# Maxima steps of 256 and 512 keys in two periods, an earlier routing block on VectorE, and late weight steps three products later

## The chip, the cores and the metric

The kernel runs on one core of one Trainium2 chip. The metric is device microseconds for one execution of the whole program; every number below is in microseconds (us) unless marked ns.

## What is computed

A routed attention feeds a two-layer network. The reference, cut to what matters:

```python
batch, n_heads, seq, head_dim = (4, 8, 768, 64);  n_clusters = 16      # attention
n_tokens, d_model, d_ff = (3072, 512, 2048)                            # network
q_assign = argmax(einsum('bhsd,hcd->bhsc', q / |q|, c / |c|))          # k_assign likewise
mask   = q_assign[:, :, :, None] == k_assign[:, :, None, :]
scores = where(mask, q @ k.T / 8, -1e9);  scores -= max(scores, axis=-1)
attn   = exp(scores) / (sum(exp(scores)) + 1e-9)
x = (attn @ v)  as (B*S, H*D)
h = x @ w_in;  g = h * erf(softplus(h));  out = g @ w_out
```

## The kernel before

**Two stages.** The attention takes a little over 400 us; the network the rest. Both are laid out so that TensorE (PE) always has a next matmul in its queue, and the order of the instructions on every engine is the order in which the Python code issues them: all engines go through a wrapper that keeps program order. Since that wrapper records every instruction, the profile gives line L62 to all of them, and they are told apart by engine and by tile names.

**Attention in periods.** The 32 heads are taken as 16 pairs `p`. One pair has 12 blocks of 128 keys by 384 queries: two halves of the queries, six key blocks each. `period(p, i)` for `i` = 0 to 5 does two of these blocks, `u` and `u+1`. In each period PE computes the float32 products of queries and keys (`products`, into the PSUM tiles `sc`, two buffers), adds the bfloat16 mask pass with the shift (`scores`, tiles `qm` and `km`), ScalarE (ACT) takes the exponential into `pr` (`curve`), GpSimd (POOL) adds up the rows (`accumulate`, into parts of `more_out`), and PE multiplies by the values (`attend`, into the PSUM tiles `turned`).

**Maxima one half pair ahead.** The shift is a bound on the row maximum, found half a pair earlier by `maxima_step`: for one block `t` of 128 queries, PE multiplies bfloat16 copies of queries and keys (`kv`, `qv`), adds the mask pass (`km`, `qm`), both into the one PSUM tile `wide`, and VectorE (DVE) reduces each row to its maximum (`nmx`). A block's 768 keys are split over two steps of 384 keys each; since two heads lie side by side, one reduction reads 768 elements. Each period has two steps. The first stands at the front of the period, before `products`; of the second, the `kv`/`qv` pass stands behind `products`, and the `km`/`qm` pass between `scores(u)` and `scores(u+1)`, on other rows of the array than these. `wide` has one buffer: a step's first matmul waits until the reduction of the step before has read it. The steps of blocks `t` = 0 and 1 of pair `p+1` fall into the periods `i` = 3 and 4 of pair `p`.

**What else VectorE has in periods 3 and 4.** In period 3, `similarities(p+2)` has PE multiply queries and keys with the cluster centres, and `choose(p+2)` turns the result into one-hot rows: a transpose into `sims`, a maximum over 16 clusters whose result goes into unused columns of the PSUM tile of block `u+1` (`sc`), and a comparison with that maximum (`hot`); the last transpose (`hotT`) follows in period 0 of the next pair. PE's products of the next period need that `sc` tile, so they wait for `hot`. In the same period stands part of a weight conversion: the network's weights arrive as 64-bit words and are turned into float32 in steps (`size_and_rest`, `bounded`, `sign`, `shifted`, `summed`). `bounded` and `shifted` are VectorE instructions over 512 elements on the same tile, `sign` is ScalarE's, `summed` GpSimd's, after which the next transfer is issued from the SyncE queue. The step `n1 = 2p - 1` passes through period 3 while it is below 22 (`N_EARLY`), that is in pairs 1 to 11. Pairs 0 to 13 have a `choose`. In period 4, `divide` has three parts for the half that has just ended: `den`, then the sum of each of two column halves `k` = 0, 1 in place in `turned`, then the product `x` that leaves for memory.

In short, VectorE's queue from the second reduction of period 3 to the first of period 4 reads, in pairs 1 to 11: reduction, `bounded`, `sims`, `shifted`, maximum, `hot`, reduction.

**The network.** Its products are made by `block`: seven products per block (a scheme with seven multiplications of half-size matrices), each four matmuls into a PSUM `bank`, of which there are six at first and eight after the last `divide`. After each product, VectorE or ScalarE adds the bank into `g`, and one entry of the list `aside_work` is issued. `hidden(0, 0)` is the first stage of the network, 28 products; its list begins with the last ten weight steps' first four (`all_weights(0, 4)`), whose data come by transfers that can start only when the attention's tiles are released; then eight GpSimd sums (`out_forms`). After its first seven products, `finish_attention` runs the last `divide`. What is left in the list at the end is issued by `finish_aside`.

Of the kernel before, what the change touches and what calls it, by code (L numbers as in the profile page):

```python
# [14 lines left out]
ALU = mybir.AluOpType  # L15
ACT = mybir.ActivationFunctionType
AX = mybir.AxisListType
PSUM = bass.MemoryType.PSUM

P = 128  # L20
B, H, S, D = 4, 8, 768, 64
# [4 lines left out]
HW = S // 2  # L26
QW = HW // 2
TW = QW + 2
HJ = NJ // 2
HP = H // 2  # L30
NPAIR = B * HP
# [39 lines left out]
def kernel(  # L71
# [125 lines left out]
    for base, pattern, sign, op, fill in (  # L197
# [5 lines left out]
            out=first, in_=first, compare_op=op, fill=fill, base=base, pattern=pattern,  # L203
# [42 lines left out]
    def bounded(n):  # L246
        w = w_steps[n][0]
        ve.tensor_scalar(out=w, in0=w, scalar1=2.0, scalar2=None, op0=ALU.max)
# [5 lines left out]
    def shifted(n):  # L254
        w = w_steps[n][0].bitcast(U32)
        ve.tensor_scalar(out=w, in0=w, scalar1=3, scalar2=None, op0=ALU.logical_shift_left)
# [8 lines left out]
    for e in range(2):  # L265
        for n in range(2):
            r = e * D + n * Q
# [112 lines left out]
    def maxima_step(p, i, sm=wide, behind=False):  # L380

        st = pairs[p]
        nmx = maxima[p % 2]
        t, half = divmod(i, 2)

        def passes(a, b, start, rows):
            for e in range(2):
                r = slice(e * D + rows.start, e * D + rows.stop)
                te.matmul(
                    sm[:, e, 0:HW], lhsT=st[a][r, t * P : (t + 1) * P],  # L390
                    rhs=st[b][r, half * HW : (half + 1) * HW], start=start, stop=not start,
                )

        passes("qv", "kv", True, slice(0, D))
        if behind:
            yield
        passes("qm", "km", False, slice(Q, D) if behind else slice(0, D))
        if behind:
            yield
        ve.tensor_reduce(  # L400
            out=nmx[:, :, t, half], in_=sm[:, :, 0:HW], axis=AX.X, op=ALU.max, negate=True
        )
        if i in (NJ - 1, 2 * NJ - 1):
            h = i // NJ
            ve.tensor_reduce(
                out=lowest[h][:, :, ::D].rearrange("p t e -> p e t"),
                in_=nmx[:, :, h * HJ : (h + 1) * HJ], axis=AX.X, op=ALU.min,
            )
            turns.append((p, h))
# [82 lines left out]
    def divide(u):  # L492

        p, half, _ = units[u]
        st = pairs[p]
        av = st["av", half]

        psum = turned[1 - half][:, 0:QW]
        for g in range(4):
            te.matmul(psum[g * Q : (g + 1) * Q], lhsT=minus, rhs=st["acc", half][:, g], start=True, stop=True)  # L500

        if u + 1 < len(units):
            inv = routep.tile([P, QW], F32, name="inv")
            den = routep.tile([P, QW], F32, name="den")
        else:
            inv, den = part_of(0, 4 * HW, QW), part_of(1, 0, QW)
        ae.activation(out=inv, in_=psum, func=ACT.Ln, bias=alleps, scale=-1.0)
        ae.activation(out=inv, in_=inv, func=ACT.Exp, scale=-1.0)
        yield
        ve.scalar_tensor_tensor(  # L510
            out=den, in0=psum, scalar=S * EPS, in1=inv, op0=ALU.subtract, op1=ALU.mult
        )
        for k in range(2):
            raw = av[:, k, 0:QW]
            ve.scalar_tensor_tensor(
                out=raw, in0=raw, scalar=av[:, k, QW : QW + 1], in1=inv, op0=ALU.add, op1=ALU.mult
            )
        yield
        x = part_of(0, (2 * p + half) % 4 * HW, HW).rearrange("p (k x) -> p k x", k=2)
        ve.scalar_tensor_tensor(  # L520
            out=x, in0=den.unsqueeze(1).to_broadcast([P, 2, QW]), scalar=2.0, in1=av[:, :, 0:QW],
            op0=ALU.add, op1=ALU.mult,
        )
        b, r = divmod(p, HP)
        for g in range(4):
            rows_of, at = r * P + g // 2 * D, b * S + half * HW + g % 2 * QW
            nc.sync.dma_start(
                out=x_dram[rows_of : rows_of + D, at : at + QW].rearrange("(k r) x -> r k x", k=2),
                in_=x[g * Q : (g + 1) * Q],
            )  # L530
        if half == 1:
            del pairs[p]
        yield
# [72 lines left out]
    aside_work = []  # L606
# [89 lines left out]
    def idle(n):  # L696
        return [lambda: None] * n
# [39 lines left out]
    def run(work):  # L737
        for _ in work:
            pass
# [13 lines left out]
    routing = [iter(())]  # L753
    part = [iter(())]

    def period(p, i):
        u = 2 * NJ * p + 2 * i
        n1, n2 = 2 * p - 1, 2 * p
        early = lambda n: 0 <= n < N_EARLY

        def mask(place):
            which = (MASKS if p else FIRST_MASKS).get((i, place))
            if which:
                return masks(p + 1, *which, turned[0 if i in (0, 5) else 1], place > 1, ve if place == 3 else ae)
            return lambda: None

        if u > 0:
            for which in turns if i in (0, 3) else ():
                turn(*which)
                turns.remove(which)  # L770
            step_ahead(u)
        mask(0)()
        next(part[0], None)
        if i == 0 and p:
            run(routing[0])
        if u == 2:
            next(routing[0])
        products(u)
        products(u + 1)
        mask(1)()  # L780
        second = step_ahead(u + 1, True) if u > 0 else iter(())
        next(second, None)
        scores(u)
        next(second, None)
        mask(3)()
        next(second, None)
        next(part[0], None)
        scores(u + 1)
        later = mask(2)
        if i == 3:  # L790
            similarities(p + 2)
            routing[0] = choose(p + 2, sc_of[u + 1][:, 0])
        curve(u)
        later()
        curve(u + 1)
        if u == 0:
            step_ahead(1)
            similarities(1)
            routing[0] = choose(1, turned[0])
            next(routing[0])  # L800
            next(routing[0])
            vectors(1, "q")
            vectors(1, "k")
        if i == 0 and early(n1 - 1):
            bounded(n1 - 1)
            shifted(n1 - 1)
            sign(n1 - 1)
        elif i == 1 and early(n1):
            size_and_rest(n1)
        elif i == 3 and early(n1):  # L810
            bounded(n1)
            sign(n1)
        elif i == 5 and early(n2):
            rest(n2)
        for _ in range(min(len(forms), FORMS.get(p, {}).get(i, 0))):
            forms.pop(0)[0]()
        if i == 3:
            next(routing[0], None)
            if early(n1):
                shifted(n1)  # L820
            for _ in range(2):
                next(routing[0], None)
        elif i == 1:
            load(p + 1, "v", v, vp)
            if p == 0:
                run(routing[0])
                transposes(2, "q")
        elif i == 2:
            transposes(p + 2, "k")
        elif i == 4:  # L830
            vectors(p + 2, "k")
            vectors(p + 2, "q")
        elif i == 5:
            transposes(p + 3, "q")
        if u > 0:
            if i == 1 and early(n1 - 1):
                summed(n1 - 1)
            elif i == 4 and early(n1):
                summed(n1)
            for w in (u - 2, u - 1):  # L840
                accumulate(w)
            if i % HJ == 1 and p in POOL_FORMS and forms:
                forms.pop(0)[1]()
            for w in (u - 2, u - 1):
                attend(w)
            if i % HJ == 0:
                part[0] = divide(u - 1)
                next(part[0])
        if i == 3 and early(n2):
            size(n2)  # L850
# [11 lines left out]
    st = pairs[0]  # L862
    st["qT"], st["kT"] = rows[0]["q"], rows[0]["k"]
    ve.transpose(out=st["qT"], in_=st.pop("q").rearrange("p n t -> p (n t)"))
    for e in range(2):
        ve.tensor_copy(
            out=ccT[e * D : (e + 1) * D, :, e * C : (e + 1) * C],
            in_=pct[e * D : (e + 1) * D].rearrange("d (r e c) -> d r e c", e=2, c=C)[:, :, e],
# [7 lines left out]
    for r in (0, D):  # L876
        for half in range(2):
            for e in range(2):
                c = r + half * Q + e * C
                ve.tensor_copy(  # L880
                    out=pick[r : r + D, half, e * D : (e + 1) * D].rearrange("p (n c) -> p n c", n=2)[:, :, 1 : C + 1],
                    in_=first[r : r + D, c : c + C].unsqueeze(1).to_broadcast([D, 2, C]),
# [70 lines left out]
    def all_weights(lo, hi):  # L953
        return sum((weights(n) for n in range(lo, hi)), [])

    out_forms = [right_forms(ge, *w_out_parts(f, 2)) for f in range(0, HF, 2)]
# [10 lines left out]
            del a[:1], b[:1]  # L967
        return work

    aside_work += all_weights(0, 4) + out_forms[0] + out_forms[1]  # L970
    hidden(0, 0, {0: finish_attention})
    finish_aside()
    aside_work += together(idle(2) + gates(0, 0, (0,)), all_weights(4, N_LATE))
# [56 lines left out]
```

## Time and profile before

| what | us |
|---|---|
| median of 3 runs (lowest, highest) | 997.0 (996.87, 997.09) |
| profiled execution: its time | 997.0 |
| profiled execution: span from first to last instruction | 995.3 |
| PE busy in the span | 987.6 |
| DVE, ACT, POOL busy | 700.5, 488.0, 350.3 |
| one pair, first `attend` of period 2 to that of the next pair (window 172.67 to 197.26) | 24.59; DVE busy 20.46 of it |
| the same for pair 12 (320.19 to 344.72) | 24.53; DVE busy 19.91 |

The time of an execution holds 1.7 us that lie around the span. Busy time of PE is modelled from overlapping matmuls, so a share of 99% says that PE is hardly ever without work, and not where it waits: short waits show in the starts of its groups. The granted clock of PE is 1.000 over the whole run.

### The profile page before, as it was taken

The numbers are of one execution on the slowest core, as the hardware profiler recorded it, in microseconds if no ns is written. First come the engines' busy times: TensorE is split into PE (matmuls) and PEld (weight loads), VectorE is DVE, ScalarE is ACT, GpSimd is POOL, SyncE is SP. The second block draws the span as 40 slices with busy tenths as digits, with TensorE's granted clock in tenths as the row PEclk, the third lists the DMA queues.
The fourth block names the chain that finished last, engine by engine and source line by source line (L and its number), as shares of the span: only waits on it lengthen the run. The fifth ranks groups of instructions, "written<-read, shape, count | busy, mean of one in ns | idle before, by whom it ended". The sixth has DMA issues, their size and how long they took to land.

```text
span 995.3 us, 20543 instructions
## 1 busy us (share of the span) xinstructions
PE 987.6 (99%) x8362; PEld 743.0 (75%) x8362; DVE 700.5 (70%) x1347; ACT 488.0 (49%) x659; POOL 350.3 (35%) x237
## 2 busy tenths in 40 slices
PE   8999999999999999999999999999999999999998
PEld 3555555555555555688888888888888888888887
DVE  8888888888888876779676554756475647655653
ACT  3777777777776665575432414150505050505050
POOL 1687878787878888662400000000000000000000
PEclk9999999999999999999999999999999999999999
DMA  9444444444444210331000100010001000000001
GB/s 223 78 110 108 107 110 111 110 113 113 87 94 110 51 35 19 102 106 65 1 12 32 42 1 22 22 43 1 22 22 43 1 21 22 1 1 22 22 1 42
DMA packets 147294, 55.88 MB, mean 56 GB/s; under 512 B 128640, under 2 KB 137088, under 8 KB 147200
## 3 DMA queue, kind: packets, MB, share of 16 engines
q1 hardware_dynamic: 144848, 54.29, 21.5%
q8 instruction: 65, 1.06, 0.4%
q10 hardware_dynamic: 2352, 0.30, 0.2%
q14 instruction: 29, 0.24, 0.1%
HBM read 41.98 MB, written 12.58 MB: 55 GB/s over the span
## 4 chain that ended last, share of the span: by engine, by line
PE 96%; DVE 1%; POOL 1%; DMA 1%; issue 0%; ACT 0%; SPq 0%; ACTq 0%; DVEq 0%; POOLq 0%
PE bank L62 43%; PE turned L62 31%; PE sc L62 16%; PE wide L62 6%; POOL more_out L62 1%; DVE nmx L62 1%; DMA g_more<-in_moe_w_out_dram 0%; DMA in_q<-in_q_dram 0%; DVE sims L62 0%; POOL x_more L62 0%; DVE kT L62 0%; DVE qT L62 0%; ACT pr L62 0%; ACT w_out L62 0%; DVE turned L62 0%
## 5 line engine op out<-in xcount | busy, mean ns | idle before, releaser
L62 POOL TENSOR_TENSOR more_out<-more_out,pr 128x768 f32<-128x768 f32 x128 | 217.0, 1695 | 19.2 <-ACT pr L62 10.5
L62 DVE TENSOR_REDUCE nmx<-wide 128x2 f32<-128x768 f32 x189 | 180.6, 955 | 58.9 <-PE wide L62 57.7
L62 ACT ACTIVATE pr<-sc 128x768 f32<-128x768 f32 x192 | 148.8, 811 | 95.6 <-PE wide L62 91.0
L62 PE MATMUL turned<-pr,in_v 128*32 128x194 f32 x3072 | 145.5, 330 | 0.0
L62 PEld LDWEIGHTS turned<-pr,in_v 128*32 128x32 f32 x3072 | 91.5, 109 | 51.2 <-issue 21.3
L62 DVE TENSOR_TENSOR g<-bank,g 128x256 f32<-128x256 f32 x222 | 89.5, 421 | 53.3 <-PE bank L62 46.4
L62 PE MATMUL bank<-x_own,w_in 128*128 128x256 f32 x424 | 104.7, 380 | 0.8 <-DVE g L62 0.8
L62 PE MATMUL bank<-w_out,g 128*128 128x256 f32 x448 | 103.1, 379 | 0.0
L62 PE MATMUL sc<-qT,kT 64*128 64x384 f32 x528 | 98.3, 484 | 0.0
L62 PEld LDWEIGHTS bank<-w_out,g 128*128 128x128 f32 x448 | 85.1, 190 | 11.6
L62 PEld LDWEIGHTS bank<-x_own,w_in 128*128 128x128 f32 x424 | 80.3, 190 | 12.6 <-DVE g L62 1.2
L62 DVE TENSOR_TENSOR osb<-bank,osb 128x256 f32<-128x256 f32 x87 | 35.4, 419 | 72.8 <-ACT osb L62 25.4
L62 ACT COPY g<-bank 128x256 f32<-128x256 f32 x28 | 10.4, 371 | 153.0 <-PE bank L62 148.5
L62 ACT ACT_TABLE_LOAD x48 | 61.6, 1283 | 45.7 <-DVE g L62 45.0
L62 PE MATMUL bank<-x_more,more_in 128*128 128x256 f32 x296 | 76.0, 379 | 0.0
L62 POOL TENSOR_TENSOR more_out<-pr,pr 128x768 f32<-128x768 f32 x32 | 60.0, 1875 | 28.4 <-ACT pr L62 28.4
L62 PEld LDWEIGHTS sc<-qT,kT 64*128 64x128 f32 x528 | 51.8, 187 | 19.8 <-ACT inv L62 2.3
L62 PE MATMUL wide<-kv,qv 64*128 64x384 bf16 x378 | 64.9, 328 | 1.1 <-ACT km L62 0.6
L62 PEld LDWEIGHTS <-qv 64*128 64x128 bf16 x384 | 26.9, 93 | 51.8 <-issue 35.7
L62 PE MATMUL bank<-more_out,g_more 128*128 128x256 f32 x272 | 64.3, 379 | 0.0
L62 DVE TENSOR_TENSOR g<-a_s,g 128x512 f32<-128x512 f32 x96 | 62.4, 688 | 1.4 <-ACT a_s L62 1.4
L62 PE MATMUL wide<-km,qm 64*128 64x384 bf16 (+1 forms) x378 | 62.5, 327 | 0.0
(170 smaller groups left out, 1667.4 us busy)
## 6 DMA issues: line engine op xcount, KB each, us to landing
x_own<-in_moe_w_in_dram SPq DMA_DIRECT2D x13, 512.0 KB, 4.2
in_v<-in_v_dram SPq DMA_DIRECT2D x32, 192.0 KB, 2.9
x_dram<-more_out SPq DMA_DIRECT2D x128, 48.0 KB, 1.9
x_own<-x_dram SPq DMA_DIRECT2D x6, 1024.0 KB, 5.0
out_dram<-osb SPq DMA_DIRECT2D x23, 256.0 KB, 2.0
in_k<-in_k_dram SPq DMA_DIRECT2D x59, 96.0 KB, 2.6
in_q<-in_q_dram SPq DMA_DIRECT2D x58, 96.0 KB, 2.6
g_more<-in_moe_w_out_dram SPq DMA_DIRECT2D x6, 512.0 KB, 3.3
```

Source lines behind the costliest of these rows:

```text
L62: ins = getattr(self.engine, name)(*args, **kw)
```

## The change

The first 256 keys, in place of 384, go to the first step and the other 512 to the second for query blocks 0 and 1 of every pair but the first; the row maxima are the same. In `divide` of a first half (`half` = 0, always in period 4), the sum of column half 1 moves behind the second maxima step of the period; `divide` of a second half is as before. In period 3 the three parts of `choose` follow one another, and `bounded` and `shifted` follow behind them; `sign` stays in its place on ScalarE. The list of `hidden(0, 0)` begins with three empty entries, so each weight step in it is issued three products later, and the last three GpSimd sums are issued after the 28th product. No instruction is added or taken away, and the queues of POOL and SP keep their order.

```diff
+FIRST_KEYS = {0: 256, 1: 256}
@@ maxima_step
         t, half = divmod(i, 2)
+        to = FIRST_KEYS.get(t, HW) if p else HW
+        keys = slice(to, S) if half else slice(0, to)
+        sm = sm[:, :, 0 : keys.stop - keys.start]
...
                 te.matmul(
-                    sm[:, e, 0:HW], lhsT=st[a][r, t * P : (t + 1) * P],
-                    rhs=st[b][r, half * HW : (half + 1) * HW], start=start, stop=not start,
+                    sm[:, e], lhsT=st[a][r, t * P : (t + 1) * P], rhs=st[b][r, keys], start=start, stop=not start,
                 )
...
         ve.tensor_reduce(
-            out=nmx[:, :, t, half], in_=sm[:, :, 0:HW], axis=AX.X, op=ALU.max, negate=True
+            out=nmx[:, :, t, half], in_=sm, axis=AX.X, op=ALU.max, negate=True
         )
@@ divide
                 out=raw, in0=raw, scalar=av[:, k, QW : QW + 1], in1=inv, op0=ALU.add, op1=ALU.mult
             )
-        yield
+            if k == half:
+                yield
@@ period
         elif i == 3 and early(n1):
-            bounded(n1)
             sign(n1)
...
         if i == 3:
-            next(routing[0], None)
+            for _ in range(3):
+                next(routing[0], None)
             if early(n1):
+                bounded(n1)
                 shifted(n1)
-            for _ in range(2):
-                next(routing[0], None)
@@ before hidden(0, 0)
-    aside_work += all_weights(0, 4) + out_forms[0] + out_forms[1]
+    aside_work += idle(3) + all_weights(0, 4) + out_forms[0] + out_forms[1]
```

## The prediction

> **What bounds the kernel now.** I read the page first, then the waits of PE, then PE and DVE in order of time in a steady pair (pair 6, 172.67 to 197.26), in pair 12, and where the network begins.
>
> ```profile
> PE 987.6 (99%) x8362; PEld 743.0 (75%) x8362; DVE 700.5 (70%) x1347; ACT 488.0 (49%) x659; POOL 350.3 (35%) x237
> PE 96%; DVE 1%; POOL 1%; DMA 1%; issue 0%; ACT 0%; SPq 0%; ACTq 0%; DVEq 0%; POOLq 0%
> ```
>
> The end is PE's: 96% of the chain. So a part of the change counts only if it shortens PE's stream, removes a wait of PE, or makes one. The sum of PE's listed waits is 4.4 us, 0.8 of them inside the network; but a matmul whose predecessor's modelled end hides the gap is not listed, so I looked at starts. Period 4 of pair 6, PE, then DVE from period 3 into period 4:
>
> ```profile
> 182.95 0.34 PE L62 MATMUL wide<-kv,qv 64*128 64x384 bf16 x2
> 183.12 0.33 PE L62 MATMUL wide<-km,qm 64*128 64x384 bf16 x2
> 183.28 1.47 PE L62 MATMUL sc<-qT,kT 64*128 64x384 f32 x8
> ...
> 184.62 0.34 PE L62 MATMUL wide<-kv,qv 64*128 64x384 bf16 x2
> ```
>
> ```profile
> 180.54 0.96 DVE L62 TENSOR_REDUCE nmx<-wide 128x2 f32<-128x768 f32 x1 [0.83 <-PE wide L62]
> 181.42 0.42 DVE L62 TENSOR_SCALAR w_in<-w_in 128x512 f32<-128x512 f32 x1
> 181.75 0.58 DVE L62 STREAM_TRANSPOSE sims<-turned 128x384 f32<-128x384 f32 x1
> 182.25 0.38 DVE L62 TENSOR_SCALAR w_in<-w_in 128x512 uint32<-128x512 uint32 x1
> 182.55 0.55 DVE L62 TENSOR_REDUCE sc<-sims 128x24 f32<-128x384 f32 x1
> 183.14 0.55 DVE L62 TENSOR_TENSOR hot<-sims,sc 128x384 bf16<-128x384 f32 x1
> 183.61 0.95 DVE L62 TENSOR_REDUCE nmx<-wide 128x2 f32<-128x768 f32 x1
> ```
>
> The first reduction was released by PE (0.83 idle before it); from there DVE runs without a gap to the reduction at 183.61, which ends at 184.56, and PE's second `wide` group starts at 184.62: 0.05 us after. In pair 12, without conversion, the products take 332.09 - 330.80 = 1.29 and not 1.34:
>
> ```profile
> 328.06 0.96 DVE L62 TENSOR_REDUCE nmx<-wide 128x2 f32<-128x768 f32 x1 [0.83 <-PE wide L62]
> 329.04 0.58 DVE L62 STREAM_TRANSPOSE sims<-turned 128x384 f32<-128x384 f32 x1
> 329.73 0.56 DVE L62 TENSOR_REDUCE sc<-sims 128x24 f32<-128x384 f32 x1
> 330.33 0.55 DVE L62 TENSOR_TENSOR hot<-sims,sc 128x384 bf16<-128x384 f32 x1
> ```
>
> So pairs 1 to 11 already lose 0.06 in period 4 (24.59 against 24.53 a pair): DVE is just late there, and this is the one place of the steady pair where PE meets DVE. The reader should also see the starts: independent neighbours start 0.08 before the end shown of the one ahead (181.42 against 180.54 + 0.96), a dependent one 0.03 after it (`hot`, 183.14), and the pair `sims`, maximum stands 0.69 apart in pair 12, 0.11 after the transpose's end.
>
> **Steps of 256 and 512, on PE.** Passes of 384 columns start 0.16 apart (183.12, 183.28), so a column costs 0.417 ns, 128 columns 0.053. The first step has two passes one after the other: -0.107. In the second step the `kv` pass stands alone: +0.053. Its `km` pass runs beside the scores on other rows, with 0.42 from its start to `attend` (180.10, 180.53): 0.21 of streaming is covered; uncovered it would be +0.053. So a period gains 0.053, if nothing waits. The shorter pass must still cover the loading of the products' float32 weights: two loads for the same rows start 108 ns apart when they are late (183.843 and 183.951 in the trace), and the pass is 107 ns: nothing, at most 0.08 a period by the row of 187 ns for such a load. I take nothing.
>
> The Trainium skill ("TensorE: Matmul & The Clock Gate", LDWEIGHTS) prices a load by its columns over 1.2 GHz, 107 ns for 128, whatever the type: by it the sum is the same as mine, by the 187 ns row 0.08 more a period where DVE isn't late anyway.
>
> **The same on DVE.** Rows of 768 and 384 elements (0.955, 0.551) give 1.05 ns an element: 512 take 0.69, 1024 take 1.22. The two together are as before, but the long one stands in front of the chain. Its start stays at 180.54: PE's second step begins 0.107 earlier, and both its passes are 0.053 longer.
>
> **Routing first.** From the 1024 reduction's start, with pair 12's spacings: 0.98 + 0.27 to `sims`, 0.69 to the maximum, 0.60 to `hot`, 0.55 to its end: 3.09 (before: 3.15). `bounded` starts 0.08 sooner, at 3.01. `bounded` and `shifted` now follow each other on one tile; in period 0 they do already, and the row below says 0.88 for both:
>
> ```profile
> 194.59 0.88 DVE L62 TENSOR_SCALAR w_in<-w_in 128x512 f32<-128x512 f32 x2
> ```
>
> They end at 3.89, the 512 reduction starts at 3.81 and ends at 4.50, where before it was 184.56 - 180.54 = 4.02. So the order costs about 0.2, two independent starts turned into dependent ones plus the wait handling at `sims`, and the long reduction 0.27, of which the short one gives its 0.27 back only at its own end: PE's second group starts at 180.54 + 4.50 + 0.05 = 185.09, 0.47 later than before, though PE could be there at 184.41. Queued behind: `den`, the reduction of the second step, `x`; the products that `hot` holds up are covered by this wait.
>
> Two more terms follow in the pair. The `kv` pass of 512 comes behind the wait: +0.05. And moving one sum behind the second reduction does let that start when PE is ready rather than behind two sums, but the sum and `x` (0.42 and 0.54, dependent) now end after it: the first reduction of period 5 starts some 0.13 later than PE allows, of which PE's slack takes about half: +0.06. Together +0.58 a pair, times 11 pairs: **+6.4**. Bounds: if a dependent start cost nothing more than an independent one, the short reduction would end at 4.02 as before: +0.11 a pair, +1.2. If `bounded` and `shifted` each pay 0.11 rather than 0.03: +0.7 a pair, +7.7. I take 0.58, since every spacing is a row of the same instructions in the same order. POOL's `summed` waits for `shifted` and comes 1.0 later, the sums behind it too; they run back to back to 193.54 and their reader, the `minus` group, starts at 194.51, so with PE itself 0.58 late 0.5 of cover is left. SP's transfers behind it are needed pairs later.
>
> The Trainium skill ("Advanced Engine Details and Errata", The Read-Write Bubble) says that the memory latency shows between any two VectorE instructions, which would make order free. The trace differs: 0.08 of overlap or a gap of 0.03 to 0.11, by dependence. By the rule the change would come to about no difference; by the rows it is slower.
>
> **Pairs without conversion.** Pairs 0, 12 and 13 have routing alone. The short reduction is ready in time (3.01 + 0.69 + 0.05 = 3.75 against PE at 3.87), but `hot` ends at 3.09 and the products' weights may load 0.12 later, at 3.20 against a natural 2.90. In pair 6 they came 0.20 late for a loss of 0.02; so 0.30 late loses 0.10, and the gain of 0.107 is gone: 0. Pair 14, no routing: -0.11. Bounds for the four: -0.43 to 0.
>
> **Late weight steps.**
>
> ```profile
> 417.23 0.66 ACT L62 ACTIVATE w_out<-g_more 128x512 f32<-128x512 f32 x1 [3.50 <-DMA g_more<-in_moe_w_out_dram]
> 417.93 0.43 DVE L62 TENSOR_SCALAR w_out<-w_out 128x512 f32<-128x512 f32 x1 [3.71 <-ACT w_out L62]
> 418.74 1.13 PE L62 MATMUL bank<-x_own,w_in 128*128 128x256 f32 x4 [0.80 <-DVE g L62]
> ```
>
> DVE's `bounded` waits for ScalarE, ScalarE for the transfer, and behind it the sums that free banks. The PE group before started at 416.81 and needs 4 x 0.216 = 0.86, so it lost 418.74 - 417.68 = 1.06. Three products later the sums of products 2 to 5 are ahead of that wait, and with eight banks after `finish_attention` the next bank needed from behind it is asked for after 420: **-1.06**. Bounds: 0 if it only moves to a later product. The three GpSimd sums left over are issued behind the 28th product and needed some 24 us later: nothing; should the steps meet POOL's sums on DVE, a row of 1.24 for `bounded` at 438.38 says +0.8 for one, hidden behind five banks of slack.
>
> **Sum** for the profiled execution of 997.0 (span 995.3), equal to the median: 997.0 + 6.4 - 0.1 - 1.06 = **1002.2**.
>
> **Rivals.**
> - *Faster, the freed buffer*: the short reduction of period 4 frees `wide` early. Place: PE's second group there; price: the wait of 0.057 goes and 0.107 is gained, 11 x 0.164 = 1.8, with 0.43 and 1.06: 993.7. It decides if the DVE stretch from the long reduction's start to the short one's end is 3.81 or less; all its rows together say 4.50, and even without dependence 4.02. Against it. 8%.
> - *No difference*: dependence costs nothing; +1.2 - 0.1 - 1.06: 997.0. For it: the work on DVE is the same; against: the gaps in pair 12. 11%.
> - *Slower still*: the wait at 417.68 only moves, or returns as one of the dependent sums in the first blocks: 1003.3. It is a part of the slower case.
> - *The change doesn't do what it says*: the order of each queue is the program's, so I leave this out.
>
> **Numbers.** A run of this kernel tells no change from 0.2%, 2.0 us. Forecast with its variants (1000.5 to 1004.4) 81%, hence slower 0.81, same 0.11, faster 0.08. The range reaches below the forecast's own towards the middle case: 999.0 to 1004.5.
>
> **What would show it.** In pairs 1 to 11, period 4: PE's second `wide` group some 0.67 behind the end of its products, the 512 reduction starting 3.8 after the 1024 one; a pair of 25.2 in place of 24.59, pair 14 alone shorter; no wait of PE near 417. Wrong if pairs 1 to 11 take 24.5 or less: then DVE doesn't set period 4; or if the network's beginning still waits.

## The result and the profile after

| | before | changed |
|---|---|---|
| median of 10 runs each (lowest, highest) | 997.10 (996.84, 997.93) | 999.77 (999.52, 1000.48) |
| ratio, 95% interval | | 1.0026 [1.0016, 1.0036] |
| span of the profiled execution | 995.3 | 998.1 |
| first to last `attend` of the attention | 384.99 | 388.82 |
| last `attend` to the last matmul | 582.03 | 580.96 |
| one pair: 1 to 11; 12 and 13; 14 | 24.59; 24.53; 23.73 | 24.97; 24.45; 23.64 |

The change costs 2.67 us, 0.26%: slower, inside the range, and about half of the 5.2 forecast. The attention gives 3.8 away, the network gets 1.07 back. Pairs 1 to 11 lose 0.38 each, where 0.58 was forecast. Pair 14 gains 0.09 (forecast: 0.11), and pairs 0, 12 and 13, for which no change was forecast, gain 0.08 to 0.09 each. Below, the time of a period runs from the start of the `attend` group before it to the start of its own.

PE in pair 6 of the changed kernel, from the first step of period 4 on (columns as before: start, duration, engine, what it writes and reads, and in brackets the idle time and what ended it):

```profile
184.73 0.28 PE L63 MATMUL wide<-kv,qv 64*128 64x256 bf16 x2
184.85 0.27 PE L63 MATMUL wide<-km,qm 64*128 64x256 bf16 x2
184.96 1.46 PE L63 MATMUL sc<-qT,kT 64*128 64x384 f32 x8
186.75 0.39 PE L63 MATMUL wide<-kv,qv 64*128 64x512 bf16 x2 [0.34 <-DVE nmx L63]
```

The two passes of 256 are 0.12 and 0.11 apart, as short as they should be. Then PE stands: the products need 1.29 of streaming (in the kernel before, 332.09 - 330.80), so the second group could start at 186.25 and starts at 186.75. The listed 0.34 is less than the 0.50 lost, since the modelled end of the last product covers the rest. VectorE shows why:

```profile
182.32 1.23 DVE L63 TENSOR_REDUCE nmx<-wide 128x2 f32<-128x1024 f32 x1 [1.15 <-PE wide L63]
183.46 0.57 DVE L63 STREAM_TRANSPOSE sims<-turned 128x384 f32<-128x384 f32 x1
184.15 0.56 DVE L63 TENSOR_REDUCE sc<-sims 128x24 f32<-128x384 f32 x1
184.74 0.56 DVE L63 TENSOR_TENSOR hot<-sims,sc 128x384 bf16<-128x384 f32 x1
185.21 0.88 DVE L63 TENSOR_SCALAR w_in<-w_in 128x512 f32<-128x512 f32 x2
186.01 0.69 DVE L63 TENSOR_REDUCE nmx<-wide 128x2 f32<-128x512 f32 x1
```

No gap but the dependent starts. The short reduction ends at 186.70, 4.38 after the long one began (before: 4.02 between the two of 384), and PE goes on 0.05 later. And the network's beginning, PE:

```profile
420.67 1.99 PE L63 MATMUL bank<-x_own,w_in 128*128 128x256 f32 x8
```

The group of four that started at 418.74 before, after a wait, now follows the four ahead of it at once: one run of eight matmuls, 1.99 for two products.

### The profile page after: what moved, and what is told of

It is laid out like the page before. It is cut to its first block, busy times and chain, and to the rows that moved or that the text cites. A ratio compares the mean times of both kernels' runs of the same rounds, so it can differ in the third digit from the quotient of the medians.

```text
span 998.1 us, 20543 instructions
## 1 busy us (share of the span) xinstructions
PE 987.5 (99%) x8362; PEld 741.5 (74%) x8362; DVE 701.8 (70%) x1347; ACT 488.0 (49%) x659; POOL 350.1 (35%) x237
## 3 DMA queue, kind: packets, MB, share of 16 engines
q8 instruction: 65, 1.06, 0.5%
## 4 chain that ended last, share of the span: by engine, by line
PE 93%; DVE 6%; issue 1%; DMA 0%; ACT 0%; DVEq 0%; SPq 0%
PE bank L63 44%; PE turned L63 29%; PE sc L63 15%; PE wide L63 5%; DVE nmx L63 2%; DVE sims L63 1%; DVE sc L63 1%; DVE w_in L63 1%; DVE hot L63 1%; DMA in_q<-in_q_dram 0%; DVE w_out L63 0%; DVE kT L63 0%; DVE qT L63 0%; DVE turned L63 0%; DVE nbig L63 0%
## 5 line engine op out<-in xcount | busy, mean ns | idle before, releaser
L63 DVE TENSOR_REDUCE nmx<-wide 128x2 f32<-128x768 f32 (+2 forms) x189 | 180.6, 956 | 60.2 <-PE wide L63 59.6
L63 PE MATMUL wide<-kv,qv 64*128 64x384 bf16 (+2 forms) x378 | 65.1, 328 | 4.8 <-DVE nmx L63 4.1
L63 PEld LDWEIGHTS <-qv 64*128 64x128 bf16 x384 | 25.2, 93 | 55.2 <-issue 38.9
L63 PE MATMUL wide<-km,qm 64*128 64x384 bf16 (+3 forms) x378 | 62.5, 327 | 0.0
```

The costliest lines, as they stand in the source:

```text
L63: ins = getattr(self.engine, name)(*args, **kw)
```

## The experiments

Each kernel was timed against the kernel before on the same chip, whose medians were 997.35 (e1 to e4), 997.04 (e5 to e7) and 997.10 (e8, e9). The theory is that of the prediction: from the second reduction of period 3, VectorE's stretch sets when PE may write `wide` again in period 4. Its rivals were that the passes of 256 and 512 cost PE time in themselves, and that VectorE's work counts wherever it stands.

**e1: the late weight steps alone**

```diff
-    aside_work += all_weights(0, 4) + out_forms[0] + out_forms[1]
+    aside_work += idle(3) + all_weights(0, 4) + out_forms[0] + out_forms[1]
```

> Only the three empty entries ahead of the weight steps of the first network stage. Theory (the wait of PE at the third bank goes and comes back nowhere): 1.06 us less than before, about 996.0; the matmuls of the network start 0.216 apart without the 1.18 gap. Rival (the part only helps because attention ends differently in the changed kernel): no change, 997.1.

Measured: 995.99, ratio 0.9987 [0.9978, 0.9997]; span 994.3 against 995.3; the pairs are as before. The wait is gone and came back nowhere; the rival falls.

**e2: the new order of routing and conversion alone**

```diff
-            bounded(n1)
             sign(n1)
...
         if i == 3:
-            next(routing[0], None)
+            for _ in range(3):
+                next(routing[0], None)
             if early(n1):
+                bounded(n1)
                 shifted(n1)
-            for _ in range(2):
-                next(routing[0], None)
```

> Only the routing block put together, bounded and shifted behind it; steps of 384 keys, divide and weight steps as before. Theory (VectorE's stretch from the second reduction of period 3 to the end of the first of period 4 releases PE, and its order alone makes it longer): the transpose starts 0.98 after the reduction (held by ScalarE's exponential), the stretch is 4.49 in place of 4.02, pairs 1 to 11 take 25.0 to 25.1 in place of 24.59, the time is 1002.3. If the transpose is free as in the changed kernel, 4.38: 1001.0. Rival (the 256 and 512 passes cost PE its time, and the order is harmless): 24.59 a pair or 24.53, 997.1 or a little less.

Measured: 1002.29, ratio 1.0050 [1.0035, 1.0065]; pairs 1 to 11 at 25.05, pairs 12 and 13 at 24.53. VectorE in pair 6:

```profile
182.86 0.96 DVE L62 TENSOR_REDUCE nmx<-wide 128x2 f32<-128x768 f32 x1 [0.83 <-PE wide L62]
183.83 0.58 DVE L62 STREAM_TRANSPOSE sims<-turned 128x384 f32<-128x384 f32 x1
184.53 0.56 DVE L62 TENSOR_REDUCE sc<-sims 128x24 f32<-128x384 f32 x1
185.12 0.55 DVE L62 TENSOR_TENSOR hot<-sims,sc 128x384 bf16<-128x384 f32 x1
185.59 0.88 DVE L62 TENSOR_SCALAR w_in<-w_in 128x512 f32<-128x512 f32 x2
186.39 0.95 DVE L62 TENSOR_REDUCE nmx<-wide 128x2 f32<-128x768 f32 x1
```

The same seven instructions with the same work as before now take 186.39 + 0.95 - 182.86 = 4.48 in place of 4.02; the order alone costs 0.46 a pair. The passes are still of 384 keys, so the rival that blames them falls. The transpose starts 0.97 after this reduction, though in the changed kernel it starts 0.09 before the end of the long one. That tells the two expectations for `sims` apart: it is not held by the reduction but by something that is ready 0.9 or so after it began. What that is, is read from pair 0 further below: PE's products for the similarities.

**e3: the steps of 256 and 512 alone.** `FIRST_KEYS` and `maxima_step` as in the change; routing, `divide` and the list of the network as before.

> Only the steps of 256 and 512 keys; routing and conversion interleaved as before, divide and weight steps as before. Theory (the long reduction pushes the routing comparison 0.27 later while PE's products come 0.16 earlier, so now the products wait for the comparison): products of period 4 split by some 0.4, pairs 1 to 11 some 0.2 longer than 24.59, pairs 12 and 13 at 24.45, time 999.0 to 999.6. Rival (without the new order the steps pay): pairs 1 to 11 at 24.5 or less, 996.

Measured: 999.45, ratio 1.0023 [1.0014, 1.0033]; pairs 1 to 11 at 24.82, pairs 12 and 13 at 24.43, pair 14 at 23.63. The time is as expected, but only a part of the loss lies where it was expected. VectorE's transpose in pair 6, and below it PE in period 4:

```profile
183.06 0.58 DVE L63 STREAM_TRANSPOSE sims<-turned 128x384 f32<-128x384 f32 x1
```

```profile
183.78 0.53 PE L63 MATMUL turned<-more_out,minus 128*32 128x192 f32 x8
184.48 1.59 PE L63 MATMUL sc<-qT,kT 64*128 64x384 f32 x8
185.87 0.41 PE L63 MATMUL wide<-kv,qv 64*128 64x512 bf16 x2
```

Period 4 takes 4.40 in pair 6 and 4.01 in pair 12, which has no conversion. The products are stretched, since their second half waits for `hot`, which ends at 185.00 in this trace: 185.87 - 184.48 = 1.39 in place of 1.29, so 0.10. The larger part lies ahead of them. The `minus` products at the start of `divide` write the PSUM tile that the transpose `sims` reads, and the transpose stands behind the long reduction and `bounded`. It ends at 183.64, `minus` starts 0.15 later, 1.54 after the first `attend` at 182.24; in pair 12 it is 332.48 - 331.17 = 1.31. That is 0.23, at a second place where PE meets VectorE, which the prediction did not have. So the new order has a use: with the long reduction in front and the old order, the transpose and `hot` are late; with the new order, the short reduction is. Either way pairs 1 to 11 lose.

**e4: the conversion in VectorE's idle time.** The changed kernel, with the two instructions in front of the second reduction of period 3:

```diff
             step_ahead(u)
+        if i == 3 and early(n1):
+            bounded(n1)
+            shifted(n1)
...
-            if early(n1):
-                bounded(n1)
-                shifted(n1)
```

> The changed kernel with bounded and shifted moved in front of the second reduction of period 3, where VectorE is idle for 1.15 us. Theory (the two conversion instructions in the stretch are all that makes pairs 1 to 11 late): those pairs become like pairs 12 and 13 of the changed kernel, 24.45; with the late weight steps 997.1 - 11 x 0.14 - 0.34 - 1.06 = 994.2, faster than both kernels. Rival (the 256 and 512 passes cost PE time in themselves, or ScalarE and GpSimd are late too): pairs 1 to 11 stay above 24.59, 996 or more.

Measured: 1006.35, ratio 1.0093 [1.0078, 1.0108]; pairs 1 to 11 at 25.56. Neither came: it is by far slower than the rival. VectorE, then GpSimd, then PE:

```profile
184.09 2.49 DVE L63 TENSOR_SCALAR w_in<-w_in 128x512 f32<-128x512 f32 x2
187.63 0.57 DVE L63 STREAM_TRANSPOSE sims<-turned 128x384 f32<-128x384 f32 x1
```

```profile
182.78 3.50 POOL L63 TENSOR_TENSOR more_out<-more_out,pr 128x768 f32<-128x768 f32 x2
```

```profile
188.34 0.53 PE L63 MATMUL turned<-more_out,minus 128*32 128x192 f32 x8 [0.87 <-DVE sims L63]
```

The pair of instructions takes 2.49 where it took 0.88 in e2, and ends at 186.58, 0.3 after GpSimd's two sums at 186.29. The idle time was no free place: GpSimd computes through it. PE meets the delay not at `wide` but at `minus`, which waits for the transpose: it starts 2.37 after the first `attend` (185.97) where it takes 1.32 in the changed kernel (184.29 - 182.97), so 1.05 of the 1.11 by which these pairs are longer than 24.45.

**e5: the conversion behind the first reduction of period 4.** As e4, but the three added lines stand in period 4 (`i == 4`), behind the first `next(part[0])`, where GpSimd waits.

> The changed kernel with bounded and shifted behind den and the first sum of period 4, where GpSimd is idle, in place of in front of the first reduction of period 4. Theory (those two instructions ahead of the reduction make PE wait, and a VectorE instruction of that kind is held only while GpSimd computes, as at 1.79 us in front of the second reduction of period 3): both take 0.43 here, period 4 falls from 4.53 to about 4.0, period 5 takes over 0.2 to 0.3 because the sums and the product of divide come late, pairs 1 to 11 take 24.65 to 24.75, time 996.3 to 997.5. Rival (VectorE's work in sum, wherever it stands, makes the pair longer): 24.97 as in the changed kernel, 999.8. Rival (the instruction in front of the second reduction was slow for another cause than GpSimd): 0.6 to 1.8 here too, over 25.2 a pair.

Measured: 1009.87, ratio 1.0130 [1.0114, 1.0145]. Period 4 takes 4.01 and period 5 takes 3.98 in place of 3.78, as expected, and both instructions take 0.88 together. But period 1 of the next pair takes 5.31 to 5.33 in place of 4.09, so pairs 1 to 11 are at 25.88. The waits of PE:

```profile
PE turned L63 <- POOL more_out L63: 11.3, 11, 1.0
PE wide L63 <- DVE nmx L63: 0.4, 2, 0.2
```

The wait for VectorE in period 4 is gone, and in its place PE waits 1.0 in each of the 11 pairs for GpSimd's sums: `summed` waits for `shifted`, and the sums of a half run back to back behind it. The cover of which the prediction said that 0.5 is left has been overdrawn. The rival on VectorE's total work falls by period 4; the time it gave was missed too, on the other side. The pair time of the second rival came, over 25.2, but not its instructions: they took 0.88 together, and not 0.6 to 1.8 each. The theory's own time was missed by 12 us, since it left out this wait for GpSimd.

**e6: `divide` as before, the rest as changed.** `yield` behind the loop, in place of `if k == half`.

> The changed kernel with both column sums of divide in front of the second step, as before. Theory (the second reduction of period 4 then starts 0.16 later than PE allows, which no matmul waits for, and period 5 gets back the 0.015 that it lost): pairs 1 to 11 at 24.95 to 24.97, time 999.5 to 999.8. Rival (the moved sum is what keeps period 4 at 4.53 and not more): 25.1 a pair, 1001.3.

Measured: 999.50, ratio 1.0026 [1.0016, 1.0036]; pairs 1 to 11 at 24.95, period 5 at 3.77 in place of 3.79. The moved sum does almost nothing, and the rival falls.

**e7: the steps of 256 and 512 in other periods**

```diff
+FIRST_KEYS = {2: 256, 3: 256, 4: 256}
+MORE_KEYS = {0: 256, 1: 256, **FIRST_KEYS}
...
+        to = (MORE_KEYS if p in (1, 13, 14, 15) else FIRST_KEYS).get(t, HW) if p else HW
```

> The kernel before with the late weight steps, and steps of 256 and 512 keys for query blocks 2, 3 and 4 (periods 5, 0 and 1) of all pairs but the first, and for blocks 0 and 1 only of pairs 1, 13, 14 and 15, whose steps meet no conversion; routing, conversion and divide as before. Theory (a period gains 0.053 wherever VectorE's reduction of 512 is done before PE's second group): 15 x 3 x 0.053 = 2.4, 0.39 in the four pairs, 1.06 in the network: 993.3, faster than both kernels. Rival (VectorE is late in periods 0 or 1 as in 4, since hotT, km, bounded and shifted stand there): pairs at 24.59 or more, 996 or more.

Measured: 1001.67, ratio 1.0046 [1.0029, 1.0063]; pairs 1 to 10 at 24.78. The theory fails and the rival's times came. Period 5 gains nothing (3.77): PE's next pass of the mask, `turned<-hotT,pick`, starts 0.23 after the `km` pass of 512 (189.41, 189.64 in pair 6), where it started 0.17 after the pass of 384 (188.66, 188.83). Period 0 loses 0.06: PE's products with `lowest` come 1.45 after the `attend` group of period 5 (191.34 - 189.89) in place of 1.34 (190.42 - 189.08), since `lowest` stands behind the long reduction and ends at 191.28. Period 2 loses 0.14: the 1024 reduction of period 1 stands behind both sums of `divide` and ends at 199.54 in pair 7, PE's first group of period 2 starts at 199.60. In pairs 12 to 14, period 1 takes 5.24. In pair 12, VectorE and then GpSimd:

```profile
319.65 2.15 DVE L64 TENSOR_TENSOR more_in<-w_in 128x512 f32<-128x512 f32 x1
```

```profile
319.43 1.82 POOL L64 TENSOR_TENSOR more_out<-pr,pr 128x768 f32<-128x768 f32 x1 [1.17 <-ACT pr L64]
```

A sum for the network that VectorE does there starts after a GpSimd sum, because the long reduction ahead of it ends later, and takes 2.15; PE's second group waits 0.98 for the reduction behind it.

**e8: only the parts that gain**

```diff
+        to = FIRST_KEYS.get(t, HW) if p in (1, 13, 14, 15) else HW
...
+    aside_work += idle(3) + all_weights(0, 4) + out_forms[0] + out_forms[1]
```

Routing, conversion and `divide` are as before.

> The kernel before with the late weight steps, and steps of 256 and 512 keys only in the maxima of pairs 1, 13, 14 and 15, which are found while no conversion stands in VectorE's stretch; routing, conversion and divide as before. Theory (the short and long steps gain 0.1 a pair only where VectorE has room): pairs 1 to 11 stay at 24.59, pairs 0, 12, 13 and 14 lose 0.1 each, the network 1.06: 997.1 - 0.39 - 1.06 = 995.6, faster than both kernels. Rival (the gain of pairs 12 to 14 hangs on the changed divide): 996.0.

Measured: 995.53, ratio 0.9985 [0.9976, 0.9994]; pairs 1 to 11 at 24.59, 12 and 13 at 24.43, 14 at 23.63. It is 0.15% faster than the kernel before, and the gain of pairs 12 to 14 is there with the old `divide`: the rival falls.

**e9: e4 with a quiet GpSimd.** The kernel leaves out GpSimd's sums of the key blocks 3, 4 and 5 of every first half.

```diff
         pr = prs[u % NPT]
+        if half == 0 and j > 2:
+            return
```

> The kernel with bounded and shifted in front of the second reduction of period 3 (1006.4, shifted 1.79), with GpSimd's sums of the key blocks 3, 4 and 5 of every first half left out, so that GpSimd is idle there; the row sums are then short of these blocks. Theory (VectorE's instruction was held by GpSimd's): bounded 0.42 and shifted 0.43, period 4 at 4.01 in pairs 1 to 11, pairs of 24.45, 994.3. Rival (the place itself is slow, by the transpose or the reductions around it): shifted stays near 1.8, pairs at 25.5, 1006.

Measured, one execution: 994.09, with all pairs from 1 to 13 at 24.44 to 24.47 and period 4 at 4.02. VectorE in pair 6:

```profile
178.50 0.88 DVE L63 TENSOR_SCALAR w_in<-w_in 128x512 f32<-128x512 f32 x2
179.73 1.23 DVE L63 TENSOR_REDUCE nmx<-wide 128x2 f32<-128x1024 f32 x1 [0.36 <-PE wide L63]
```

In the same place both instructions take 0.88, and there is 0.36 of idle time left behind them. So e4's 2.49 was GpSimd's doing, and with the conversion out of the stretch pairs 1 to 11 are like pairs 12 and 13: the theory holds to 0.02 us a pair. That it is the place of the two instructions, and not the quiet GpSimd, which makes period 4 short, is shown by e5: with GpSimd's sums in place and the two instructions out of the stretch, period 4 takes 4.01.

## Why the prediction was right, and where its sizes were off

- **DVE sets period 4 in pairs 1 to 11**: right, shown from both sides. Order alone makes them 25.05 (e2); with the two instructions out of the stretch period 4 falls from 4.53 to 4.01 (e5) and the pairs to 24.45 (e9). The signs came in kind and not in size: the 512 reduction starts 3.69 after the 1024 one (3.8 forecast), PE's second group stands 0.50 behind its products (0.67), a pair takes 24.97 (25.2). That this is "the one place" where PE meets DVE is not so: `minus` behind `sims` is another. In the kernel before, `minus` starts 0.18 after `sims` ends, and 0.15 in e3 and e4, where it waits, so the room was 0.03.
- **The price, 0.58 a pair**: the mechanism was right and the term too large; it measured 24.97 - 24.59 = 0.38. Three sizes were off. First and largest, the start of `sims`, "0.98 + 0.27", 1.25 after the long reduction began: it measured 183.46 - 182.32 = 1.14, and the stretch 4.38 in place of 4.50. The 0.98 was the wait for another engine, and it does not grow with the reduction: in the changed kernel that engine is done before the long reduction ends, and the transpose starts 0.09 ahead of the reduction's end like any independent neighbour. The transpose waits for two engines in the program, PE (the similarities) and ScalarE, and in pair 12 before both end at the same time: PE's products at 328.05 + 0.85 = 328.90, the exponential of block `u` at 328.89, the transpose starts at 329.04. Pair 0 of the kernel before tells them apart. ScalarE, then PE and VectorE:

```profile
33.03 0.81 ACT L62 ACTIVATE pr<-sc 128x768 f32<-128x768 f32 x1 [1.17 <-PE wide L62]
```

```profile
33.06 0.85 PE L62 MATMUL turned<-more_out,ccT 128*32 128x384 f32 x8
34.05 0.58 DVE L62 STREAM_TRANSPOSE sims<-turned 128x384 f32<-128x384 f32 x1
```

Here ScalarE is done 0.20 before the transpose, and PE again 0.14 before it; e1 and e2 show the same two spacings in their pair 0. So it was PE's products that held the transpose, and not ScalarE's exponential, as was expected for e2. In the changed kernel they end at 182.30 + 0.85 = 183.15, before the long reduction does. Second, "its start stays": the long reduction starts 0.44 after its `km` pass of 512 (181.88, 182.32), as it did after the pass of 384 (180.10, 180.54), so the gain of 0.05 in period 3 stays. Third, period 5 became 0.015 longer and not 0.06. Together 0.12 + 0.05 + 0.045 = 0.215, against 0.58 - 0.38 = 0.20.
- **The split of the 0.47, order 0.2 and long reduction 0.27**: wrong, and its own rows say so. With reductions of 384 keys the same spacings, 0.98 + 0.69 + 0.60 + 0.47 + 0.80 + 0.95 (0.47 and 0.80 are 0.55 and 0.88 less the overlap of 0.08), already make 4.49 in place of 4.02. e2 measured 4.48: the order alone costs 0.46. With steps of 256 and 512 it is 4.38: the long reduction adds nothing to the stretch and takes 0.10 off it, since it covers the transpose's wait.
- **Pairs without conversion, 0 and -0.11**: pair 14 became 0.09 shorter, and pairs 0, 12 and 13 became 0.08 to 0.09 shorter where nothing was expected, against the sign "pair 14 alone shorter": `hot` came 0.11 earlier than reckoned, for the same reason, so the products hardly waited. Four pairs: -0.34 in place of -0.11.
- **The 256 pass covers the weights' loading**: right; the passes start 0.11 to 0.12 apart and the products follow at once.
- **Late weight steps, -1.06**: measured -1.07 in the changed kernel and 1.0 of span in e1. The rival by which the wait only moves falls with e1.
- **The sum**: 11 x 0.38 - 0.34 - 1.06 = 2.8, against 2.67 between the medians. The measured 999.77 lies below the forecast's own variants, 1000.5 to 1004.4; it is inside the range because that was drawn down towards the middle case. The direction and the place were reckoned; that the range holds owes something to its margin.
- **The rival of the early buffer**: its point was a stretch of 3.81 or less; it is 4.38. The middle rival, by which order is free, falls with e2: 4.48 against 4.02 for the same work.

## What to carry to other kernels

Where one engine's short chain releases another, price the chain by starts, not by durations, and ask of each spacing whether it belongs to the instruction or to a wait for a third engine: only the first kind moves along when the chain is changed. VectorE's idle time was a place for work only while GpSimd was idle too (e4, e9), and only if nothing on a third queue waits for what is moved (e5). A change of several parts is worth taking apart: here the late weight steps and the short steps of four pairs gain about 1.5 us together (e8), and the same steps with the new order in pairs 1 to 11 cost 4.2.

## What the runs showed of the hardware

VectorE instructions of two forms (one tensor and a constant, all in SBUF; two tensors in SBUF) were held by GpSimd's. In e4 the two conversion instructions end 0.28 and 0.29 after a GpSimd sum ends (184.75 after 184.47, 186.58 after 186.29), and e9 shows that the sums are the cause. The trace of before had it already, in the network's first stage, first VectorE, then GpSimd:

```profile
438.38 1.24 DVE L62 TENSOR_SCALAR w_out<-w_out 128x512 f32<-128x512 f32 x1
```

```profile
438.07 1.27 POOL L62 TENSOR_TENSOR more_out<-w_out,more_out 128x512 f32<-128x512 f32 x1
```

It ends 0.28 after the GpSimd instruction beside it, where the same instruction takes 0.42 alone. The sum of two tensors in e7 ends 0.55 after GpSimd's (319.65 + 2.15 = 321.80 after 321.25). In the kernel before, the same sum starts first and takes 0.68, and GpSimd's takes 2.31 in place of 1.82:

```profile
317.52 0.68 DVE L62 TENSOR_TENSOR more_in<-w_in 128x512 f32<-128x512 f32 x1
```

```profile
317.56 2.31 POOL L62 TENSOR_TENSOR more_out<-pr,pr 128x768 f32<-128x768 f32 x1 [1.11 <-ACT pr L62]
```

The Trainium skill ("SBUF — State Buffer", Who interferes with whom) says that the two engines share a port pair that goes whole to the one that comes first; the rows agree, and they add the 0.28 and the 0.55.

Two lesser things: a second pass of 512 columns beside the scores on other rows cost no more than one of 384 (period 3 takes 4.54 in place of 4.59, the gain of 0.05 that the passes alone would give), unless a further pass follows it as in e7's period 5; and two VectorE instructions of which one needs the other's result cost 0.12 more than two that don't (in e9 `bounded` starts 0.085 before the end of the reduction ahead, `shifted` 0.034 after the end of `bounded`).
